# Mamba2 scan and SiLU feed-forward on one core: weight pieces taken up one to three slots ahead, first unit's scan and transposes reordered, one unit's load issued earlier

## Chip, cores and metric

The kernel runs on one core of a Trainium2 chip. The engines are TensorE (PE, matmuls and transposes), VectorE (DVE), ScalarE (ACT), GpSimd (POOL) and SyncE (SP, which issues most loads and stores). The metric is the device time of one execution in microseconds (us); lower is better.

## Reference

```python
# attention: batch 4, heads 8, seq 768, head_dim 32, d_state 16
cum = np.cumsum(log(clip(a)), axis=-1)             # within a chunk
L   = exp(cum[:, None] - cum[None, :]) * causal
y   = ((C @ B.T) * L) @ x + (C @ state) * exp(cum)  # intra + inter chunk
state = exp(sum(la)) * state + sum_j (B_j x_j) * exp(cum_last - cum_j)
# bridge: (batch, heads, seq, head_dim) -> 3072 tokens x 256
h = x @ w_in                                        # 256 x 2048
g = h * (1 / (1 + exp(-h)))                         # SiLU
out = g @ w_out                                     # 2048 x 256
```

Everything is in fp32. The result does not depend on the chunk length, and the kernel uses 64.

## The kernel before

The 3072 tokens are 12 units of 256 (three to a batch entry, `UPB = 3`). A unit first goes through the scan and gives `XM`, the transposed attention output; then through the feed-forward part in slots. `f_s1(g, j)` is a slot of eight fp32 matmul instructions of unit g with two column blocks of w_in, and a silu on ACT that writes `gT`. `f_s2(g, j)` is a slot of eight matmul instructions with w_out, which wants pieces 8 + 2(j mod 4) and 9 + 2(j mod 4) of the weights. In the main loop, group g does `f_s1(g, j)`, one step of the scan of unit g + 1, and `f_s2(g - 2, j)`.

The scan of a unit has these steps: `f_P` (prefix scan of the decays over pa: DVE, POOL, DVE), `f_E` (decay matrix E by one long DVE scan over ab, or for units 0 and 1 `f_Ek`, from a broadcast of ach by matmuls), `f_T` (four PE transposes of B and C into one hp tile, evicted by ACT as bh and ce and by DVE as cw), `f_B` (B times decay, POOL), `f_GD` (grams on PE, then M, the states st and sp on DVE), `f_Y` (output on PE, XM on ACT).

The weights come in 16 pieces of 512 KB, eight of w_in and eight of w_out, through eight raw buffers, and each goes through three steps before it is used: `w_size` (two ACT operations, wu and wv), `w_bits` (two DVE operations on wu, then an add on POOL into wv) and `w_sign` (one DVE operation that writes w_in_sb or w_out_sb, after which SP may issue the load of the piece eight further on). Slot j of f_s1 wants piece j.

Each engine runs its instructions in the order in which the code writes them (the schedule is manual), and the tile framework adds the waits. Two PSUM buffers hold the hp tiles, which f_s1, f_T and the idle matmuls of `busy(n)` share in turn: a third tile waits for the readers of the first. SP issues loads and stores in the order written: after the first loads of units 0, 1 and 2 and of eight pieces come the other eight pieces, then what the main loop asks for (`load_unit`, and the outputs of `f_s2`).

The order around the change is written by hand: a sequence for units 0 and 1, a table `steps` for groups 0 and 1, whose letters s, b and g stand for w_size, w_bits and w_sign of a piece, and three lines in the main loop for group 2:

```python
f_s2(g - LAG, j)
for n in range(2 * j + 10, 2 * j + 12):
    if g == 2 and n < len(W):
        w_size(n)
        w_bits(n)
        w_sign(n)
```

Of the kernel before, what the change touches and what calls it, by code (L numbers as in the profile page):

```python
# [509 lines left out]
```

## Time and profile before

| | before |
|---|---|
| time, median of 3 runs | 430.13 us (429.73 to 430.16) |
| the profiled execution | 429.28 us, of which the span is 427.6 |
| PE busy | 397.3 us, 93% of the span |
| DVE, ACT, POOL busy | 105.9, 105.3, 35.4 us |
| mean granted clock of TensorE | 0.976 |

The span is from the first to the last instruction of the profiled execution. PE busy is no measure of PE at its best, since matmuls are pipelined and their ends are modelled, and a matmul at half clock is busy for twice as long. So stretches of time and the waits in them say more than the shares.

### The profile page before, as it was taken

How to read it: one execution, taken by the hardware profiler on the slowest of the kernel's cores; microseconds unless marked ns; L12 is line 12 of the kernel's file. 1: busy time of each engine (PE TensorE's matmuls, PEld its weight loads, DVE VectorE, ACT ScalarE, POOL GpSimd, SP SyncE). 2: the span in 40 equal slices, each digit the busy share in tenths (PEclk: the TensorE clock that was granted, in tenths of full speed). 3: DMA queues.
4: the chain of work that ended last, by engine and by line, in shares of the span. 5: the costliest groups of instructions: out<-in, count | busy, mean ns of one | idle time of the engine just before them, and what ended most of it. 6: DMA issues, size and time to landing. Idle time of an engine off the chain costs nothing.

```text
span 427.6 us, 7947 instructions
## 1 busy us (share of the span) xinstructions
PE 397.3 (93%) x3478; PEld 328.1 (77%) x3478; DVE 105.9 (25%) x187; ACT 105.3 (25%) x202; POOL 35.4 (8%) x74
## 2 busy tenths in 40 slices
PE   8964998769959999999999999999999999999996
PEld 3443786548838888888888888888888888888885
DVE  5552146543245005005005014023032020000000
ACT  1332355532211222121221222222222222221000
POOL 3122041440000000000000000000000000000000
PEclk9896699999989999999999999999999999999999
DMA  9995149000096044053061071080080000000101
GB/s 174 248 193 165 49 148 161 3 1 14 18 144 81 8 87 51 2 92 44 2 107 30 2 114 24 8 117 14 16 111 14 12 2 14 12 14 0 26 12 25
DMA packets 105966, 25.18 MB, mean 59 GB/s; under 512 B 97228, under 2 KB 101836, under 8 KB 105932
## 3 DMA queue, kind: packets, MB, share of 16 engines
q1 hardware_dynamic: 101772, 24.42, 30.7%
q10 hardware_dynamic: 4160, 0.26, 0.7%
q8 instruction: 27, 0.44, 0.5%
q14 instruction: 7, 0.06, 0.1%
HBM read 21.52 MB, written 3.15 MB: 58 GB/s over the span
## 4 chain that ended last, share of the span: by engine, by line
PE 86%; DVE 5%; POOL 3%; DMA 1%; issue 1%; SPq 1%; ACT 1%; POOLq 0%; ACTq 0%
PE o_ps L391 38%; PE hp L380 37%; POOL wv L154 3%; PE hp L194 2%; PE gy L363 2%; PE gy L306 2%; PE gy L354 1%; PE o_ps L257 1%; DVE w_out_sb L159 1%; PE hp L282 1%; PE gy L312 1%; DVE wu L153 1%; DVE M L317 1%; DMA bct<-in_C_dram 1%; DVE wu L151 1%
## 5 line engine op out<-in xcount | busy, mean ns | idle before, releaser
L380 PE MATMUL hp<-XM,w_in_sb 128*128 128x256 f32 x768 | 185.6, 388 | 11.2 <-DVE w_in_sb L159 10.2
L391 PE MATMUL o_ps<-w_out_sb,gT 128*128 128x256 f32 x768 | 183.3, 384 | 6.9 <-DVE w_out_sb L159 6.7
L380 PEld LDWEIGHTS hp<-XM,w_in_sb 128*128 128x128 f32 x768 | 149.2, 195 | 33.3 <-issue 9.4
L391 PEld LDWEIGHTS o_ps<-w_out_sb,gT 128*128 128x128 f32 x768 | 144.2, 191 | 29.7 <-DVE w_out_sb L159 9.7
L382 ACT ACTIVATE gT<-hp 128x512 f32<-128x512 f32 x96 | 57.3, 597 | 236.3 <-PE hp L380 236.3
L292 DVE TENSOR_TENSOR cw<-hp,pfx 128x256 f32<-128x256 f32 x12 | 5.1, 422 | 149.1 <-ACT ce L291 149.0
L154 POOL TENSOR_TENSOR wv<-wu,wv 128x512 uint32<-128x512 uint32 x16 | 20.2, 1266 | 54.1 <-DVE wu L153 45.5
L250 DVE TENSOR_TENSOR_SCAN E<-ab,diag 128x1024 f32<-128x1024 f32 x10 | 22.9, 2292 | 2.2 <-POOL ab L267 2.2
L317 DVE TENSOR_TENSOR M<-gy,E 128x1024 f32<-128x1024 f32 x12 | 14.7, 1224 | 30.6 <-PE gy L312 30.6
L396 ACT ACTIVATE o_sb<-o_ps 128x256 f32<-128x256 f32 x24 | 9.2, 383 | 52.5 <-PE o_ps L391 52.5
L244 POOL COPY pb<-pa 128x4 f32<-128x4 f32 x12 | 2.3, 191 | 190.6 <-DVE pa L242 190.6
L282 PE MATMUL hp<-ident,bct 128*128 128x128 f32 x48 | 8.6, 297 | 5.0 <-DMA bct<-in_B_dram 4.9
L194 PE MATMUL hp<-idle 128*128 128x512 bf16 x30 | 11.6, 547 | 1.3 <-DVE idle L189 1.3
L282 PEld LDWEIGHTS hp<-ident,bct 128*128 128x128 f32 x48 | 6.4, 150 | 8.1 <-issue 5.5
L334 DVE SCALAR_TENSOR_TENSOR st<-st,pfx,gy 128x64 f32<-128x64 f32 x40 | 11.2, 279 | 1.1
L354 PEld LDWEIGHTS gy<-cw,sp 32*64 32x64 f32 x352 | 6.3, 133 | 6.3 <-issue 5.1
L143 ACT ACTIVATE wu<-raw 128x512 f32<-128x512 f32 x16 | 10.7, 667 | 0.0
L145 ACT ACTIVATE wv<-raw 128x512 f32<-128x512 uint32 x16 | 10.6, 664 | 0.0
L247 DVE TENSOR_TENSOR_SCAN pfx<-pa,pb 128x256 f32<-128x256 f32 x12 | 9.2, 767 | 5.4 <-POOL pa L245 5.4
L369 ACT ACTIVATE XM<-gy 128x512 f32<-128x512 f32 x12 | 7.2, 597 | 13.0 <-PE gy L363 13.0
L363 PE MATMUL gy<-M,xt 64*32 64x64 f32 x768 | 10.3, 224 | 0.0
L291 ACT ACTIVATE ce<-hp,par 128x256 f32<-128x256 f32 x24 | 10.0, 477 | 0.0
(44 smaller groups left out, 117.0 us busy)
## 6 DMA issues: line engine op xcount, KB each, us to landing
ab<-in_a_dram SPq DMA_DIRECT2D x40, 128.0 KB
raw<-in_moe_w_in_dram SPq DMA_DIRECT2D x8, 512.0 KB
raw<-in_moe_w_out_dram SPq DMA_DIRECT2D x8, 512.0 KB
xt<-in_x_dram SPq DMA_DIRECT2D x24, 128.0 KB
out_dram<-o_sb SPq DMA_DIRECT2D x48, 64.0 KB
pa<-in_a_dram SPq DMA_DIRECT2D x12, 128.0 KB
...
```

The source lines that it names most:

```text
L143: nc.scalar.activation(u, raw[n][:, :, :, 1].bitcast(FP32), AF.Abs)
L145: nc.scalar.activation(v, raw[n][:, :, :, 0], AF.Copy, scale=2.0 ** -51, bias=2.0)
L154: nc.gpsimd.tensor_tensor(out=v, in0=u, in1=v, op=ALU.add)
L194: nc.tensor.matmul(out=t, lhsT=idle[:, 0:128], rhs=idle, start=True, stop=True)
L250: nc.vector.tensor_tensor_scan(out=E[u][:, k:k + n].rearrange("p k h t -> p (k h t)"), data0=t, data1=diag[:, 0:n * H].rearrange("p g t -> ...
L282: nc.tensor.transpose(out=tp[:, 2 * i + k], in_=bct[u][:, i, k].rearrange("p h n -> p (h n)"), identity=ident)
L317: nc.vector.tensor_tensor(out=M[u].rearrange("p k g x -> p g k x"), in0=gram[:, :, 0:256].rearrange("p g (k x) -> p g k x", k=2), in1=E[u] ...
L334: nc.vector.scalar_tensor_tensor(out=o, in0=ST[u][:, t], scalar=PFX[u][:, Q * t + Q - 1:Q * t + Q], in1=d, op0=ALU.mult, op1=ALU.add)
L363: nc.tensor.matmul(out=y[32 * q:32 * q + 32, 2 * w + c, 64 * k:64 * k + 64], lhsT=xc[64 * c:64 * c + 64, k, h], rhs=m[64 * c:64 * c + 64, ...
L380: nc.tensor.matmul(out=hp[:, i], lhsT=w_in_sb[:, kc, f * 128:(f + 1) * 128], rhs=xm[:, kc], start=(kc == 0), stop=(kc == KC - 1))
L382: nc.scalar.activation(GTS[g][:, 2 * j:2 * j + 2], hp, AF.Silu)
L391: nc.tensor.matmul(out=OPS[g], lhsT=GTS[g][:, f, 128 * c:128 * c + 128], rhs=w_out_sb[:, f, :], start=(f == 0), stop=(f == NF - 1))
```

## The change

The steps of a piece are written in different slots: the ACT step one to three slots ahead of the sign step, from the table `steps` (now with f_s1 of units 0 and 1 in turn) to the first three slots of group 2 (`late`). f_GD is split into f_G (grams and M) and f_S (states), cw is taken out of f_T as f_C, and the broadcast matmuls out of f_Ek as f_Ab. For unit 0 the prefix scan stands ahead of the scans of E, and the transposes right behind the broadcast matmuls, with fewer idle matmuls (19 instead of 30). ach and sel lie on rows 96 to 107 with zeros in front, so that the broadcast matmuls take 108 rows instead of 12. Unit 3's load is issued before group 2, and unit 4's in slot 2 of it, where it was in slot 7. The scan of unit 3 has its steps in slots 1, 2, 3 and 6 of group 2, where they were in 4 to 7.

```diff
@@ -163,8 +163,9 @@
             load_w(n + RAW, nc.sync)
-    ach = const.tile([S // Q, H, Q], FP32, name="ach")
-    nc.sync.dma_start(out=ach, in_=bass.AP(tensor=a.tensor, offset=a.offset, ap=[[Q, S // Q], [S, H], [1, Q]]))
+    A0, A1 = 96, 96 + S // Q
+    ach = const.tile([128, H, Q], FP32, name="ach")
+    nc.sync.dma_start(out=ach[A0:A1], in_=bass.AP(tensor=a.tensor, offset=a.offset, ap=[[Q, S // Q], [S, H], [1, Q]]))
     load_bc(0, 0, nc.scalar)
     load_bc(0, 1, nc.scalar)
     load_pa(0, nc.sync)
...
@@ -193,11 +194,12 @@
         for i in range(n):
             nc.tensor.matmul(out=t, lhsT=idle[:, 0:128], rhs=idle, start=True, stop=True)
-    sel = const.tile([S // Q, 4, 2, 64], FP32, name="sel")
+    nc.vector.memset(ach[0:A0], 0.0)
+    sel = const.tile([128, 4, 2, 64], FP32, name="sel")
     nc.gpsimd.memset(sel, 0.0)
     nc.gpsimd.affine_select(out=sel, in_=sel, pattern=[[-2, 4], [-1, 2], [0, 64]], compare_op=ALU.not_equal,
-                            fill=1.0, base=0, channel_multiplier=1)
+                            fill=1.0, base=-A0, channel_multiplier=1)
     diag1 = const.tile([128, 1, Q], FP32, name="diag1")
     nc.vector.memset(diag1, 0.0)
...
@@ -251,15 +253,17 @@
                                      data1=diag[:, 0:n * H].rearrange("p g t -> p (g t)"),
                                      initial=0.0, op0=ALU.mult, op1=ALU.add)
+    def f_Ab(u, k):
+        ab[u, k] = t = ps_o.tile([128, H, Q], FP32, name="o_ps")
+        nc.tensor.matmul(out=t.rearrange("p h t -> p (h t)"),
+                         lhsT=sel[:A1, 2 * u + k].rearrange("r c m -> r (c m)"),
+                         rhs=ach[:A1].rearrange("r h t -> r (h t)"), start=True, stop=True)
     def f_Ek(u, k):
-        t = ps_o.tile([128, H, Q], FP32, name="o_ps")
-        nc.tensor.matmul(out=t.rearrange("p h t -> p (h t)"),
-                         lhsT=sel[:, 2 * u + k].rearrange("r c m -> r (c m)"),
-                         rhs=ach.rearrange("r h t -> r (h t)"), start=True, stop=True)
         if k == 0:
             E[u] = sc.tile([128, 2, H, Q], FP32, name="E")
-        scan_E(u, k, 1, t.rearrange("p h t -> p (h t)"))
+        scan_E(u, k, 1, ab.pop((u, k)).rearrange("p h t -> p (h t)"))
     def f_E(u):
         t = ab.pop(u)
...
@@ -289,9 +293,12 @@
         nc.scalar.activation(BH[u], tb, AF.Copy)
         for e in range(2):
             nc.scalar.activation(CE[u][:, e], tcc, AF.Copy, scale=par[:, e:e + 1])
-        nc.vector.tensor_tensor(out=CW[u], in0=tcc, in1=PFX[u], op=ALU.mult)
-    def f_GD(u):
+        TC[u] = tcc
+    def f_C(u):
+        nc.vector.tensor_tensor(out=CW[u], in0=TC.pop(u), in1=PFX[u], op=ALU.mult)
+    def f_G(u):
         first, last = u % UPB == 0, u % UPB == UPB - 1
         bh, ce = BH.pop(u), CE.pop(u)
...
@@ -319,7 +326,13 @@
                                 in1=E[u].rearrange("p k (g e) t -> p g k (e t)", e=2), op=ALU.mult)
         E.pop(u)
         bct.pop(u)
+        DP[u] = gram
+    def f_S(u):
+        first, last = u % UPB == 0, u % UPB == UPB - 1
+        n = 3 if last else 4
+        gram = DP.pop(u)
         if first:
             ST[u] = sc.tile([128, 4, 64], FP32, name="st")
         if not last:
...
@@ -404,75 +417,83 @@
             f_E(u)
         elif plan[j] == "T":
             f_T(u)
+            f_C(u)
             f_B(u)
         elif plan[j] == "G":
-            f_GD(u)
+            f_G(u)
+            f_S(u)
         elif plan[j] == "Y":
             f_Y(u)
+    f_Ab(0, 0)
+    f_Ab(0, 1)
+    f_P(0)
     f_Ek(0, 0)
     f_Ek(0, 1)
+    f_T(0)
+    f_C(0)
+    f_B(0)
+    w_size(0)
+    w_size(1)
+    f_G(0)
+    f_Ab(1, 0)
+    f_Ab(1, 1)
+    w_bits(0)
+    f_S(0)
     busy(6)
-    f_P(0)
-    f_T(0)
-    f_B(0)
+    f_Y(0)
+    w_sign(0)
     busy(4)
-    f_GD(0)
-    w_size(0)
-    w_bits(0)
-    busy(8)
-    f_Y(0)
-    w_size(1)
-    f_Ek(1, 0)
-    busy(6)
-    w_sign(0)
     f_s1(0, 0)
     w_bits(1)
+    f_Ek(1, 0)
+    w_sign(1)
     f_Ek(1, 1)
-    w_sign(1)
+    f_T(1)
+    w_size(2)
+    f_s1(0, 1)
     f_P(1)
-    f_T(1)
+    f_C(1)
     f_B(1)
-    f_s1(0, 1)
-    w_size(2)
-    f_GD(1)
     w_bits(2)
+    w_size(3)
+    f_G(1)
     w_sign(2)
+    busy(4)
     f_s1(0, 2)
-    w_size(3)
+    f_S(1)
     w_bits(3)
+    f_Y(1)
     w_sign(3)
-    f_Y(1)
-    f_s1(0, 3)
-    steps = ((1, 0, "s4"), (1, 1, "b4 s5"), (1, 2, "g4 b5 s6"), (1, 3, "g5 b6 s7"), (0, 4, "g6 b7"), (1, 4, "g7"),
-             (0, 5, ""), (1, 5, ""), (0, 6, "E"), (1, 6, "T s8"), (0, 7, "G b8 s9"), (1, 7, "g8 b9 Y"))
-    for g, j, todo in steps:
-        f_s1(g, j)
+    steps = ((1, 0, "s4"), (1, 1, "b4 s5"), (1, 2, "g4 b5 s6"), (0, 3, "g5 b6 s7"), (1, 3, "g6 b7 s8"),
+             (0, 4, "g7 b8 E"), (1, 4, "g8 s9"), (0, 5, "T b9"), (1, 5, "g9 s10"), (0, 6, "G b10"),
+             (1, 6, "g10 s11"), (0, 7, "Y b11"), (1, 7, "g11 s12"))
+    def w_steps(todo):
         for step in todo.split():
             if step[0] in "sbg":
                 {"s": w_size, "b": w_bits, "g": w_sign}[step[0]](int(step[1:]))
             else:
                 scan_piece(2, 0, step)
-    w_sign(9)
+    for g, j, todo in steps:
+        f_s1(g, j)
+        w_steps(todo)
+    load_unit(3)
+    late = ("b12 g12 s13 b13", "g13 s14 b14", "g14 s15 b15 g15")
     for g in range(2, NU + LAG):
         for j in range(8):
             if g < NU:
                 f_s1(g, j)
             if g + 1 < NU:
-                scan_piece(g + 1, j, ("", "", "", "", "E", "T", "G", "Y") if g == 2 else
+                scan_piece(g + 1, j, ("", "E", "T", "G", "", "", "Y", "") if g == 2 else
                            ("E", "T", "G", "", "", "Y", "", ""))
             f_s2(g - LAG, j)
-            for n in range(2 * j + 10, 2 * j + 12):
-                if g == 2 and n < len(W):
-                    w_size(n)
-                    w_bits(n)
-                    w_sign(n)
+            if g == 2 and j < len(late):
+                w_steps(late[j])
             if g == 2 and j == 2:
-                load_unit(3)
-            if g == 2 and j == 7:
                 load_unit(4)
             if j == 7 and g + 3 < NU:
                 load_unit(g + 3)
```

DVE's rows from the bits step of piece 7 on, in the kernel before (wu, wv and raw are the tiles of a piece, the unit is 2):

```order
L153 TENSOR_SCALAR wu_571<-wu_571 128x512
L159 SCALAR_TENSOR_TENSOR w_in_sb_90<-raw_128,wv_572 128x2x256
L242 TENSOR_SCALAR pa_130<-pa_130 128x256
L247 SCALAR_TENSOR_TENSOR pfx_617<-pa_130,pb0_187 128x256
L266 TENSOR_SCALAR ab_132<-ab_132 128x1024
L250 SCALAR_TENSOR_TENSOR E_621<-ab_132,diag_176 128x1024
L292 TENSOR_TENSOR cw_636<-hp_629,pfx_617 128x256
L317 TENSOR_TENSOR M_682<-gy_653,E_621 128x4x2x128
L334 SCALAR_TENSOR_TENSOR st_433<-st_433,pfx_617,gy_653 128x64 x3
L339 TENSOR_TENSOR sp_687<-st_433,hmask_185 128x256
L151 TENSOR_SCALAR wu_643<-wu_643 128x512
```

The same place in the changed kernel, from the bits step of piece 8 on:

```order
L153 TENSOR_SCALAR wu_570<-wu_570 128x512
L244 TENSOR_SCALAR pa_130<-pa_130 128x256
L249 SCALAR_TENSOR_TENSOR pfx_589<-pa_130,pb0_187 128x256
L270 TENSOR_SCALAR ab_132<-ab_132 128x1024
L252 SCALAR_TENSOR_TENSOR E_593<-ab_132,diag_176 128x1024
L159 SCALAR_TENSOR_TENSOR w_out_sb_91<-raw_330,wv_571 128x512
L299 TENSOR_TENSOR cw_619<-hp_612,pfx_589 128x256
L151 TENSOR_SCALAR wu_602<-wu_602 128x512
L153 TENSOR_SCALAR wu_602<-wu_602 128x512
L159 SCALAR_TENSOR_TENSOR w_out_sb_91<-raw_350,wv_603 128x512
L324 TENSOR_TENSOR M_675<-gy_646,E_593 128x4x2x128
```

The steps of unit 2 stood together behind piece 7 and in front of the bits of piece 8; now pieces 8 and 9 stand between them, with the scan of E in front of the sign of piece 8 and cw behind it.

PE's rows around the transposes of unit 2 (hp is the tile of a slot of f_s1 or of the transposes) in the kernel before:

```order
L380 MATMUL hp_608<-XM_333,w_in_sb_90 128x256 x4
L380 MATMUL hp_623<-XM_511,w_in_sb_90 128x256 x4
L282 MATMUL hp_629<-ident_160,bct_137 128x128 x4
L380 MATMUL hp_647<-XM_333,w_in_sb_90 128x256 x4
L306 MATMUL gy_653<-ce_635,bh_634 64x128 x16
```

And in the changed kernel:

```order
L393 MATMUL hp_606<-XM_327,w_in_sb_90 128x256 x4
L286 MATMUL hp_612<-ident_161,bct_137 128x128 x4
L393 MATMUL hp_629<-XM_497,w_in_sb_90 128x256 x4
L393 MATMUL hp_640<-XM_327,w_in_sb_90 128x256 x4
L313 MATMUL gy_646<-ce_618,bh_617 64x128 x16
```

There was one slot between the transposes and the grams; now there are two, the second of which, f_s1(0, 6), takes the buffer that the transposes had.

SP's loads and stores from the loads of unit 3 on, change against before:

```order
 L98 DMA bct<-in_C_dram 128x8x16 x2
 L105 DMA xt<-in_x_dram 128x8x32 x2
-L399 DMA out_dram<-o_sb 64x256 x4
 L80 DMA pa<-in_a_dram 128x1x256
 L89 DMA ab<-in_a_dram 64x8x64 x4
```

The four stores of group 2's output stood between the loads of unit 3 and those of unit 4; now they stand behind those of unit 4.

## Rows read from the trace of the kernel before

**Rows 1.** Waits of PE: engine, line, who ended them; us in total, times, longest

```profile
PE hp L380 <- DVE w_in_sb L159: 10.2, 3, 5.9
PE o_ps L391 <- DVE w_out_sb L159: 6.7, 5, 1.8
PE hp L282 <- DMA bct<-in_B_dram: 4.9, 2, 4.2
```

**Rows 2.** Windows: us, each engine's busy us (instructions), PEclk, DMA share, GB/s

```profile
18.95:22.36 3.41, 3.41 (x9) 1.87 (x8) 2.52 (x4) 0.60 (x2) 0.71 (x1) 0.50 1.04 389
32.60:39.43 6.83, 3.83 (x12) 2.69 (x16) 1.38 (x3) 0.04 (x1) 1.26 (x1) 0.50 0.71 243
...
42.84:49.67 6.83, 5.93 (x14) 4.81 (x15) 0.69 (x1) 0.60 (x1) 0.03 (x1) 0.50 0.25 77
...
124.76:128.17 3.41, 3.27 (x9) 2.41 (x9) 2.26 (x2) 1.11 (x3) 0.64 (x1) 0.50 0.88 172
128.69:159.57 30.88, 30.88 (x294) 26.54 (x293) 6.69 (x11) 7.15 (x14) 1.06 (x4) 1.00 0.34 56
128.69:427.60 298.91, 294.79 (x2517) 254.00 (x2515) 49.28 (x80) 62.02 (x121) 7.43 (x28) 1.00 0.23 37
```

**Rows 3.** The chain that ended last, one slot: start us, us, what

```profile
97.30 1.73 PE hp L380 x8
```

**Rows 4.** Timeline of the head: start us, us, engine, line, operation [idle before <-releaser]

```profile
2.72 0.41 DVE L184 TENSOR_SCALAR ach<-ach 12x512 f32<-12x512 f32 x1 [1.30 <-DMA ach<-in_a_dram]
...
3.93 3.78 PE L257 MATMUL o_ps<-ach,sel 12*128 12x512 f32 x4
...
10.17 1.06 PE L282 MATMUL hp<-ident,bct 128*128 128x128 f32 x4
...
13.73 1.22 DVE L317 TENSOR_TENSOR M<-gy,E 128x1024 f32<-128x1024 f32 x1 [0.90 <-PE gy L312]
...
16.22 0.42 DVE L151 TENSOR_SCALAR wu<-wu 128x512 f32<-128x512 f32 x1
...
17.85 0.60 ACT L369 ACTIVATE XM<-gy 128x512 f32<-128x512 f32 x1 [4.35 <-PE gy L363]
...
21.23 2.45 PE L380 MATMUL hp<-XM,w_in_sb 128*128 128x256 f32 x8
```

**Rows 5.** Timeline: PE at f_s1(0, 2) and f_s1(0, 3)

```profile
35.59 3.75 PE L380 MATMUL hp<-XM,w_in_sb 128*128 128x256 f32 x8 [5.90 <-DVE w_in_sb L159]
...
43.74 1.62 PE L380 MATMUL hp<-XM,w_in_sb 128*128 128x256 f32 x3 [2.94 <-DVE w_in_sb L159]
```

**Rows 6.** Timeline: one piece of w_out in group 2, and the next one's bits

```profile
75.01 0.42 DVE L151 TENSOR_SCALAR wu<-wu 128x512 f32<-128x512 f32 x1
...
76.03 1.26 POOL L154 TENSOR_TENSOR wv<-wu,wv 128x512 uint32<-128x512 uint32 x1 [1.67 <-DVE wu L153]
...
77.33 0.69 DVE L159 SCALAR_TENSOR_TENSOR w_out_sb<-raw,wv 128x512 uint32<-128x512 uint32 x1 [1.44 <-POOL wv L154]
...
77.94 0.42 DVE L151 TENSOR_SCALAR wu<-wu 128x512 f32<-128x512 f32 x1
```

**Rows 7.** Timeline around the loads of unit 4 (SPq is SP's queue)

```profile
115.90 0.67 SPq L80 DMA_DIRECT2D pa<-in_a_dram  x1
...
117.54 1.89 PE L380 MATMUL hp<-XM,w_in_sb 128*128 128x256 f32 x8
...
123.64 0.30 PE L282 MATMUL hp<-ident,bct 128*128 128x128 f32 x1 [4.21 <-DMA bct<-in_B_dram]
...
128.69 1.89 PE L380 MATMUL hp<-XM,w_in_sb 128*128 128x256 f32 x8
```

**Rows 8.** The page's costliest groups: the first ACT step (busy us, mean ns)

```profile
L143 ACT ACTIVATE wu<-raw 128x512 f32<-128x512 f32 x16 | 10.7, 667 | 0.0
```

**Rows 9.** Timeline: prefix scan and E of unit 3 on DVE, without weights beside it

```profile
96.03 0.29 DVE L242 TENSOR_SCALAR pa<-pa 128x256 f32<-128x256 f32 x1
...
98.26 2.29 DVE L250 TENSOR_TENSOR_SCAN E<-ab,diag 128x1024 f32<-128x1024 f32 x1 [0.22 <-POOL ab L267]
```

More of the change, by code (lines that the diff above doesn't have):

```diff
@@ L183, in f_A @@
     def f_A():
-        nc.vector.tensor_scalar(out=ach, in0=ach, scalar1=1.0, scalar2=1e-6, op0=ALU.min, op1=ALU.max)
-        nc.vector.memset(ach[:, :, 0:1], 0.0)
+        nc.vector.tensor_scalar(out=ach[A0:A1], in0=ach[A0:A1], scalar1=1.0, scalar2=1e-6, op0=ALU.min, op1=ALU.max)
+        nc.vector.memset(ach[A0:A1, :, 0:1], 0.0)
     idle = const.tile([128, 512], BF16, name="idle")
@@ L210 @@
     nc.scalar.activation(tiny, idle[:, 0:1], AF.Silu)
-    busy(6)
+    busy(5)
     f_A()
@@ L234 @@
         pb.append(t)
-    E, M, BT, BH, CE, CW, PFX, ST, DP, XM, GTS, OPS = ({} for _ in range(12))
+    E, M, BT, BH, CE, CW, PFX, ST, DP, XM, GTS, OPS, TC = ({} for _ in range(13))
     def f_P(u):
@@ L406, in scan_piece @@
             f_T(u)
+            f_C(u)
             f_B(u)
         elif plan[j] == "G":
-            f_GD(u)
+            f_G(u)
+            f_S(u)
         elif plan[j] == "Y":
             f_Y(u)
+    f_Ab(0, 0)
+    f_Ab(0, 1)
+    f_P(0)
     f_Ek(0, 0)
     f_Ek(0, 1)
+    f_T(0)
[8 more added lines that the diff above has]
+    f_S(0)
     busy(6)
-    f_P(0)
-    f_T(0)
-    f_B(0)
+    f_Y(0)
+    w_sign(0)
     busy(4)
-    f_GD(0)
-    w_size(0)
-    w_bits(0)
-    busy(8)
-    f_Y(0)
-    w_size(1)
-    f_Ek(1, 0)
-    busy(6)
-    w_sign(0)
     f_s1(0, 0)
     w_bits(1)
+    f_Ek(1, 0)
+    w_sign(1)
     f_Ek(1, 1)
-    w_sign(1)
+    f_T(1)
+    w_size(2)
+    f_s1(0, 1)
     f_P(1)
-    f_T(1)
+    f_C(1)
     f_B(1)
-    f_s1(0, 1)
-    w_size(2)
-    f_GD(1)
     w_bits(2)
+    w_size(3)
+    f_G(1)
     w_sign(2)
+    busy(4)
     f_s1(0, 2)
-    w_size(3)
+    f_S(1)
     w_bits(3)
+    f_Y(1)
     w_sign(3)
-    f_Y(1)
-    f_s1(0, 3)
-    steps = ((1, 0, "s4"), (1, 1, "b4 s5"), (1, 2, "g4 b5 s6"), (1, 3, "g5 b6 s7"), (0, 4, "g6 b7"), (1, 4, "g7"),
-             (0, 5, ""), (1, 5, ""), (0, 6, "E"), (1, 6, "T s8"), (0, 7, "G b8 s9"), (1, 7, "g8 b9 Y"))
-    for g, j, todo in steps:
-        f_s1(g, j)
+    steps = ((1, 0, "s4"), (1, 1, "b4 s5"), (1, 2, "g4 b5 s6"), (0, 3, "g5 b6 s7"), (1, 3, "g6 b7 s8"),
+             (0, 4, "g7 b8 E"), (1, 4, "g8 s9"), (0, 5, "T b9"), (1, 5, "g9 s10"), (0, 6, "G b10"),
+             (1, 6, "g10 s11"), (0, 7, "Y b11"), (1, 7, "g11 s12"))
+    def w_steps(todo):
         for step in todo.split():
```

## Prediction

> **What bounds the kernel now.** I read the page first: TensorE (PE) is busy 93% of a 427.6 us span, so what is left to gain is PE's waits and the stretches in which it runs slowly. Next the waits of PE [rows 1]: 10.2 us for w_in_sb, 6.7 for w_out_sb, and 4.9 for the B load of one unit. Then the windows with the granted clock [rows 2]: 0.50 (1.2 GHz) from 32.60 to 39.43, from 42.84 to 49.67 and from 124.76 to 128.17, each beginning during or right after one of these waits. From 128.69 on the kernel is steady: a unit takes 30.88 us, and 298.91 are left [rows 2]. A slot (eight matmuls) takes 1.73 [rows 3], so the scan steps of a unit cost 30.88 - 16 x 1.73 = 3.2 on PE. All that the change can move lies before 128.69, and the question is when the changed kernel reaches the work that starts there, f_s1(3, 2).
>
> Before that point three places lose time. The head: the first slot starts at 21.23 [rows 4]. The weights: f_s1(0, 2) waits 5.90 and then takes 3.75, f_s1(0, 3) waits 2.94 [rows 5]; in group 2 the slots stand in a cycle of VectorE (DVE) and GpSimd (POOL) for each piece of w_out: bits at 75.01, POOL's add at 76.03, sign at 77.33, the next bits at 77.94 [rows 6], 2.93 a piece. Unit 4: its loads are issued at 115.90, its transposes start at 123.64 although PE's slot of 117.54 was over at 119.3, and the next regular slot starts at 128.69 instead of 117.54 + 2 x 1.73 + 0.44 = 121.4 [rows 7]: 7.2 lost.
>
> **The change, part by part.**
>
> Unit 4's load moves from group 2, slot 7 to slot 2, and unit 3's ahead of group 2. Both then stand on SP's queue in front of group 2's outputs, behind the eight pieces of w_out, the last of which waits for sign 7. By the chain below sign 7 is done at T0 + 15, so both are in long before they are read (unit 4's loads took 8 from issue to first use [rows 7]). Gain 7.2; between 0, if they came late all the same, and 7.2. I take 7.2, since the queue's order settles it.
>
> The head. The transposes of unit 0 move in front of two runs of matmuls on idle data and now follow the two broadcast matmuls of ach. They start between 7.3 (the end of those matmuls less one idle matmul) and 10.17, as now [rows 4]; I take 8.0, near the lower bound, because at 10.17 they wait for no load. From there to M is 3.56 [rows 4], so M starts near 11.5. From M to XM's start is 4.1, and XM takes 0.6 [rows 4]; the bits of piece 0 (0.9 [rows 6]) now stand between M and the state steps, so f_s1(0, 0) starts near 11.5 + 4.1 + 0.65 + 0.9 = 17.2, four earlier than 21.23. The memset of 96 rows of ach lies in the 1.30 that DVE waits for ach's load [rows 4]; were it longer than this wait, the excess would count. The broadcast matmuls read 108 rows where they read 12. No row shows that form; nothing here suggests that rows cost time, and its columns are the same, so 0, or at the most a doubling of about 1 each on a stretch that is no longer the last to end.
>
> From f_s1(0, 0) to the first slot after f_Y(1). Now that is 21.23 to 43.74, 22.5. Of this 10.2 are waits [rows 1], about 2.0 the slow slot at 35.59 (3.75 for 1.73), 0.5 the slow first one, 1.0 the two ach matmuls, which move forward; 0.9 of idle matmuls are new: 9.7 of work. What waits remain? Behind sign 0 DVE has bits 1, scan E, sign 1, scan E, the prefix scan, cw, bits 2, M, sign 2: 0.9 + 1.2 + 0.6 + 1.2 + 1.4 + 0.4 + 0.9 + 1.1 + 0.6 = 8.3. Sign 0 ends near 15.5, so piece 2 is there near 24.5, and PE comes near 23.4: a wait of 1.2; then 0.8 for XM of unit 1. With 9.7 + 2.0 this first slot, T0, starts at 17.2 + 11.7 = 28.9. All this is at full clock. The present head has half rate for long stretches, and the new one has fewer idle matmuls and still short gaps, so I add one stretch at half rate, 1.5: T0 = 30.4 (27.5 with none and a quick head, 33 with three).
>
> Pieces 4 to 15. The three steps of a piece are now in different slots, but look at the order on DVE: sign n stands in front of bits n+1 everywhere, so POOL's add of n+1 cannot start before sign n is done. The cycle is the one of [rows 6], 2.93, whatever slot the steps are written in, and DVE, not PE at 1.73 a slot, paces it. Bits 4 need the first slot (1.73), a silu and the first ACT step, 0.67 [rows 8]: T0 + 3.1. From bits 4 to sign 15's release are 11 cycles and the end of one: 11 x 2.93 + 2.3 + 0.75 = 35.3. Into this row DVE must fit, without PE's help: the prefix scan and E of units 2 and 3, each 4.45 from pa to the end of E (96.03 to 98.26 and 2.2 more [rows 9]), plus 1.0 because POOL's copy for it stands behind an add, less the 1.4 that DVE would have waited for that add: 4.05 each; cw of unit 2, 0.35; M and the states of unit 2, 2.5 (13.73 to 16.22 [rows 4]) and 0.2 of waiting for them. Sum 3.1 + 35.3 + 8.1 + 0.35 + 2.7 = 49.6: the second half of f_s2(0, 3) can run at T0 + 49.6.
>
> Where PE then stands. f_T(2) takes one of two hp buffers; f_s1(0, 6), two tiles on, needs it back, so it waits for cw of unit 2, which stands on DVE behind E of unit 2 and sign 8. PE is there at T0 + 9 x 1.73 + 0.8 = T0 + 16.4; sign 8 starts at 3.1 + 4 x 2.93 + 2.3 + 4.05 = T0 + 21.2, cw is through at 22.3. That is a new wait of 6.0, which the present kernel does not have, since it puts E of unit 2 two slots before the transposes and no weights beside it. It ends in time for DVE's cycle, so it is no term of its own. It brings half rate, though: the present wait of 5.90 was followed by a slot of 3.75 [rows 5] at 0.50 [rows 2]. M of unit 2, on DVE's row, stands behind that slot and the grams, so I add 2.0 (0 if the clock holds, 3.4 if it is low for both).
>
> The Trainium skill (TensorE: Matmul & The Clock Gate, the section on HAM oscillation) says that waits between groups of matmuls put the array back to half rate again and again; it speaks against taking idle matmuls out of the head. [rows 2] agree as far as they go. By it the whole head would run low: the second rival.
>
> **Sum.** After T0 + 49.6 there are half a slot (0.87), 12 slots (20.7), f_Y(3) and f_T(4) with their switches (2.2) to f_s1(3, 2): T0 + 73.4. With T0 = 30.4 and 2.0 for the clock that is 105.8, where the present kernel has 128.69: 22.9 less. Span 105.8 + 298.9 = 404.7. The profiled execution took 429.28 for a span of 427.6, 1.7 around it: 406.4. Its own time lies 0.85 under the median of the runs shown, 430.13, so I say 406.
>
> **Rivals.**
>
> PE bounds it all (10%). If the slot-apart steps do hide the cycle, PE runs from T0 to f_s1(3, 2) without waits: 33 slots (57.0), scans of units 2 and 3 (6.4) and f_T(4) (0.44), 63.9. Then 30.4 + 63.9 + 298.9 + 1.7 = 395, or 393 with no slow stretch. For it: ACT and SP have room, and loads are early. Against it: sign n in front of bits n+1 in DVE's row.
>
> The clock stays at half to 29 us (8%). From the transposes at 8.0 to T0 PE has about 16 of work (three slots 5.2; transposes, grams and outputs of two units 5.7; ach 2.1; 14 idle matmuls 3.0), so far partly beside DVE's. At half rate it becomes the path: with 2 of waits, 9.5 of it are done by 29 and the rest by about 36 to 37. Time 37 + 73.4 + 2.0 + 298.9 + 1.7 = 413. For it: three stretches of 0.50 [rows 2], and eleven idle matmuls fewer. Against it: shorter waits, and four of these are put where PE would wait for piece 2.
>
> Unit 4 still waits for its loads (3%): 406 + 7.2 = 413.
>
> Not faster (2%): the clock stays at half well into group 2. By the same count T0 would be 8 + 2 + 32 = 42. A slot at half rate takes 3.45, longer than DVE's cycle, so PE is the bound: by 80 us it would have done 19 of the 63.9 that follow T0 (the count of the first rival), and the other 45 at full rate, with the last waits for pieces 13 and 15, end at 128, where the present kernel is at that point. So 80 us is where it decides; lower clock for longer is slower than now, and the price is half a microsecond for each at half rate. Against it: in the present profile no stretch after the head is longer than 6.83 [rows 2], and all end once PE runs without gaps.
>
> **How the numbers follow.** The DVE-paced case has 77%, with 399 (T0 27.5, no clock loss: 27.5 + 73.4 + 300.6 = 401.5, and 2 for head steps that I took too long) to 413 (T0 33, 3.4 lost, 2 for steps that I took too short). This range takes in most of the two cases at 413 and leaves out the PE-bound one and the slow one. 0.2% is about what a measurement of this kernel can tell from no change: faster 0.97, same 0.01, slower 0.02.
>
> **What would show it.** Right: the waits of PE name one of 5 to 7 for f_s1(0, 6) ended by cw on DVE, just behind a long E scan; bits of consecutive pieces 2.9 apart from piece 4 on and two gaps of about 7 between pieces 8 and 9 and 13 and 14; no wait for bct; f_s1(3, 2) near 106 and 299 from there to the end. Wrong: pieces less than 2.5 apart (then near 395); a clock of 0.50 over most of the first 30 us (413 or more); a wait of ACT for raw, behind which silu and then PE would stand.

## The result and the profile after

The changed kernel takes **406.85 us** (median of 4 runs, 405.85 to 407.87); the kernel before, run beside it, 429.93 (427.68 to 430.16). The ratio is 0.947 (95% interval 0.943 to 0.951): 23.1 us less, and 0.85 over the 406 predicted. The profiled execution is the longest of the four: 407.87 for a span of 406.2.

From the page of the changed kernel:

```profile
span 406.2 us, 7918 instructions
```

The waits of PE in the changed kernel, which answer to [rows 1] (L393 is f_s1, L404 f_s2, L286 the transposes, L299 cw, L159 the sign step):

```profile
PE hp L393 <- DVE cw L299: 5.7, 1, 5.7
PE o_ps L404 <- DVE w_out_sb L159: 2.7, 2, 1.4
PE hp L286 <- DMA bct<-in_C_dram: 2.0, 1, 2.0
...
PE hp L393 <- DVE w_in_sb L159: 1.1, 1, 1.1
```

The waits for w_in fell from 10.2 to 1.1, those for w_out from 6.7 to 2.7, the wait for B of unit 4 is gone; a wait of 5.7 for cw of unit 2 and one of 2.0 for C of unit 0 are new.

The timeline of the changed kernel at the places that the prediction named. They answer, in order, to [rows 4], [rows 5], [rows 6], [rows 9] and [rows 7]:

```profile
3.56 2.50 PE L259 MATMUL o_ps<-ach,sel 108*128 108x512 f32 x4
...
8.68 0.33 PE L286 MATMUL hp<-ident,bct 128*128 128x128 f32 x1 [1.96 <-DMA bct<-in_C_dram]
...
14.57 1.63 PE L195 MATMUL hp<-idle 128*128 128x512 bf16 x6
...
18.30 1.89 PE L393 MATMUL hp<-XM,w_in_sb 128*128 128x256 f32 x8
...
30.94 14.08 PE L393 MATMUL hp<-XM,w_in_sb 128*128 128x256 f32 x64 [0.74 <-ACT XM L382]
...
40.09 0.42 DVE L151 TENSOR_SCALAR wu<-wu 128x512 f32<-128x512 f32 x1
...
41.15 1.27 POOL L154 TENSOR_TENSOR wv<-wu,wv 128x512 uint32<-128x512 uint32 x1 [1.70 <-ACT wu L143]
...
42.45 0.69 DVE L159 SCALAR_TENSOR_TENSOR w_in_sb<-raw,wv 128x512 uint32<-128x512 uint32 x1 [1.47 <-POOL wv L154]
43.06 0.42 DVE L151 TENSOR_SCALAR wu<-wu 128x512 f32<-128x512 f32 x1
...
50.17 2.29 DVE L252 TENSOR_TENSOR_SCAN E<-ab,diag 128x1024 f32<-128x1024 f32 x1 [0.22 <-POOL ab L271]
...
52.96 0.42 DVE L299 TENSOR_TENSOR cw<-hp,pfx 128x256 f32<-128x256 f32 x1
...
53.43 3.78 PE L393 MATMUL hp<-XM,w_in_sb 128*128 128x256 f32 x8 [5.72 <-DVE cw L299]
...
83.67 1.13 PE L404 MATMUL o_ps<-w_out_sb,gT 128*128 128x256 f32 x4 [1.36 <-DVE w_out_sb L159]
...
105.12 0.60 PE L286 MATMUL hp<-ident,bct 128*128 128x128 f32 x4
...
107.28 1.89 PE L393 MATMUL hp<-XM,w_in_sb 128*128 128x256 f32 x8
```

Read it from below. f_s1(3, 2) starts at 107.28 and not at 128.69 [rows 7], 21.41 earlier; the profiled executions differ by the same 21.41 (429.28 and 407.87), so all of the gain was made before it, and the steady part is unchanged. T0, the first slot behind f_Y(1), is 30.94; the kernel before has 43.74 there [rows 5]. So 12.80 come from the head, and 8.61 from the stretch between T0 and f_s1(3, 2) (84.95 before, 76.34 after). The head takes in weight pieces 0 to 3: all waits for w_in in the kernel before lie in it, and 9.1 of the 12.80 are what these waits fell by (10.2 to 1.1).

The windows of the changed kernel: us, each engine's busy us (instructions), PEclk, DMA share, GB/s.

```profile
11.49:14.90 3.41, 3.41 (x5) 0.98 (x5) 3.27 (x8) 1.24 (x2) 1.26 (x1) 0.50 0.84 95
...
52.45:59.27 6.82, 5.84 (x65) 4.15 (x66) 2.81 (x7) 0.60 (x1) 2.21 (x2) 0.50 0.86 112
```

Two stretches at 0.50 (1.2 GHz) are left where [rows 2] had four; the second follows the wait for cw.

### The profile page after: what moved, and what is told of

It reads as the page before. It is cut to its first block, busy times and chain, and to the rows that moved or that the text cites. A ratio compares the mean times of both kernels' runs of the same rounds, so it can differ in the third digit from the quotient of the medians.

```text
span 406.2 us, 7918 instructions
## 1 busy us (share of the span) xinstructions
PE 386.2 (95%) x3467; PEld 323.6 (80%) x3467; DVE 106.1 (26%) x188; ACT 105.5 (26%) x202; POOL 35.7 (9%) x74
## 4 chain that ended last, share of the span: by engine, by line
PE 84%; DVE 5%; POOL 3%; issue 3%; ACT 2%; DMA 1%; ACTq 0%; POOLq 0%; DVEq 0%
PE o_ps L404 40%; PE hp L393 35%; POOL wv L154 3%; PE gy L376 2%; PE gy L313 2%; PE gy L367 2%; DMA bct<-in_C_dram 1%; DVE w_out_sb L159 1%; PE gy L319 1%; PE hp L286 1%; DVE wu L153 1%; PE o_ps L259 1%; ACT wu L143 1%; DVE wu L151 1%; PE hp L195 1%
## 5 line engine op out<-in xcount | busy, mean ns | idle before, releaser
L393 PE MATMUL hp<-XM,w_in_sb 128*128 128x256 f32 x768 | 182.7, 383 | 8.1 <-DVE cw L299 5.7
L404 PE MATMUL o_ps<-w_out_sb,gT 128*128 128x256 f32 x768 | 181.2, 382 | 2.7 <-DVE w_out_sb L159 2.7
L393 PEld LDWEIGHTS hp<-XM,w_in_sb 128*128 128x128 f32 x768 | 146.6, 192 | 29.9 <-DVE cw L299 6.1
L404 PEld LDWEIGHTS o_ps<-w_out_sb,gT 128*128 128x128 f32 x768 | 143.6, 190 | 23.5 <-DVE w_out_sb L159 3.5
L299 DVE TENSOR_TENSOR cw<-hp,pfx 128x256 f32<-128x256 f32 x12 | 5.1, 423 | 160.7 <-ACT ce L295 160.7
L145 ACT ACTIVATE wv<-raw 128x512 f32<-128x512 uint32 x16 | 10.7, 671 | 0.0
L278 POOL TENSOR_TENSOR BT<-bct,E 128x256 f32<-128x256 f32 x12 | 8.0, 667 | 25.2 <-DVE E L252 17.8
L313 PEld LDWEIGHTS gy<-ce,bh 32*64 32x64 f32 x384 | 5.7, 138 | 5.4 <-issue 4.0
L313 PE MATMUL gy<-ce,bh 32*64 32x128 f32 x384 | 8.8, 293 | 1.2 <-ACT ce L295 1.2
L376 PEld LDWEIGHTS gy<-M,xt 64*32 64x32 f32 x768 | 8.4, 105 | 1.6 <-issue 0.8
```

Of the source, the lines that this page charges most:

```text
L145: nc.scalar.activation(v, raw[n][:, :, :, 0], AF.Copy, scale=2.0 ** -51, bias=2.0)
L313: nc.tensor.matmul(out=gram[64 * c:64 * c + 64, g, 128 * k:128 * k + 128], lhsT=bh[32 * g:32 * g + 32, ts], rhs=ce[32 * g:32 * g + 32, :, ts],
L376: nc.tensor.matmul(out=y[32 * q:32 * q + 32, 2 * w + c, 64 * k:64 * k + 64], lhsT=xc[64 * c:64 * c + 64, k, h], rhs=m[64 * c:64 * c + 64, ...
L393: nc.tensor.matmul(out=hp[:, i], lhsT=w_in_sb[:, kc, f * 128:(f + 1) * 128], rhs=xm[:, kc], start=(kc == 0), stop=(kc == KC - 1))
L404: nc.tensor.matmul(out=OPS[g], lhsT=GTS[g][:, f, 128 * c:128 * c + 128], rhs=w_out_sb[:, f, :], start=(f == 0), stop=(f == NF - 1))
```

## The experiments

Each is an edit of the changed kernel (of the kernel before where it says so). Medians are compared with 406.85; the kernel before, run beside them, gave medians of 428.9 to 430.1 and single runs of 424.5 to 432.3. The changed kernel's four runs are all from one time. So a difference of 1 to 2.5 us between medians of four to six runs says little by itself, and beside it stands the same stretch in the traces: T0 to f_s1(3, 2), 76.34 in the changed kernel.

**1. Unit 4 loaded late again.**

```diff
-            if g == 2 and j == 2:
+            if g == 2 and j == 7:
                 load_unit(4)
```

> The changed kernel, with the loads of unit 4 put back to slot 7 of group 2. Theory (the place of these loads is worth 7.2 us): 414 us, with a wait of PE of 4 to 5 us for B or C of unit 4 and half rate behind it. Rival (the loads would be hidden anyway, the gain came from elsewhere): 407 us and no such wait.

415.84 (415.14 to 416.57), ratio 0.970 (0.964 to 0.976) to the kernel before: 9.0 lost, not 7.2. Timeline, then one window of this kernel:

```profile
110.19 0.45 PE L286 MATMUL hp<-ident,bct 128*128 128x128 f32 x1 [4.16 <-DMA bct<-in_B_dram]
...
112.27 3.62 PE L404 MATMUL o_ps<-w_out_sb,gT 128*128 128x256 f32 x8
```

```profile
109.43:116.26 6.83, 5.53 (x14) 4.00 (x15) 3.41 (x3) 1.11 (x3) 0.76 (x2) 0.50 0.85 148
```

Half rate held for 6.83 about the wait, against 3.41 in the kernel before [rows 2], so that a slot took 3.62. The profiled execution is 8.70 longer than that of the changed kernel, of which 0.75 lie in front of the wait (the slot before it starts at 104.14, in the changed kernel at 103.39): 7.95 are the load's.

**2. The kernel before, with unit 4 loaded early and nothing else.**

```diff
             if g == 2 and j == 2:
                 load_unit(3)
-            if g == 2 and j == 7:
                 load_unit(4)
```

> The kernel before, with the load of unit 4 issued right behind that of unit 3 (at g = 2, j = 2), and nothing else of the change. Theory: the wait of the transposes of unit 4 and the half clock behind it are a gain by themselves, whatever the rest of the change does: late issue in the changed kernel cost 9.0 us (415.84 against 406.85), so early issue alone takes the kernel before from 429.0 to 420 to 422. Rival: in the kernel before, these loads queue on SP behind loads of weights still under way and come no earlier, or the weights come later by it: 427 or more.

422.12 (417.21 to 423.05), ratio 0.984 (0.975 to 0.992): 6.8 less than the 428.91 beside it. The theory, which gave 420 to 422, holds but for 0.1. The timeline of this kernel, T0 and f_s1(3, 2):

```profile
44.84 5.46 PE L380 MATMUL hp<-XM,w_in_sb 128*128 128x256 f32 x12 [2.99 <-DVE w_in_sb L159]
...
122.45 1.89 PE L380 MATMUL hp<-XM,w_in_sb 128*128 128x256 f32 x8
```

From T0 to f_s1(3, 2) it takes 77.61; the changed kernel takes 76.34. So of the 8.61 won there 7.34 are the load of unit 4, and only **1.3 is left for all else that changed behind T0**: the pieces from 4 on taken up ahead and the scans of units 2 and 3 moved. By experiment 1 it is less: with the late load the changed kernel takes 84.38, the kernel before 84.95. What pieces 0 to 3 won is part of the head.

**3. The old head.** The code of the kernel before up to f_Y(1), without f_s1(0, 3), then the steps of the changed kernel; ach stays on 108 rows.

> The changed kernel with the head of the kernel before (units 0 and 1 up to Y of unit 1, with weight pieces 0 to 3 in their old places), then the steps of the changed kernel from slot (1, 0) on. Theory: the first slot behind Y of unit 1 comes at 43.7 as in the kernel before and not at 30.9, all else stays: 406.9 + 12.8 = 419.7, up to 3.4 more if the clock stays at half for the stretch behind it as before. Rival: the pieces, whose loads are there earlier against this later start, then run ahead of PE and the wait of 5.7 for cw of unit 2 goes too: 412 to 415.

414.99 (414.71 to 415.2): 8.1 more, within the 412 to 415 of the rival; but the wait for cw, which the rival had go, is still 5.7, so it came out right for another reason. Two waits of PE in this kernel, then its timeline, with T0 in the last row:

```profile
PE hp L393 <- DVE w_in_sb L159: 8.1, 3, 5.9
PE hp L393 <- DVE cw L299: 5.7, 1, 5.7
```

```profile
3.48 2.79 PE L259 MATMUL o_ps<-ach,sel 108*128 108x512 f32 x4
...
32.19 3.75 PE L393 MATMUL hp<-XM,w_in_sb 128*128 128x256 f32 x8 [5.90 <-DVE w_in_sb L159]
...
38.26 14.08 PE L393 MATMUL hp<-XM,w_in_sb 128*128 128x256 f32 x64 [0.90 <-ACT XM L382]
```

T0 came 7.3 later than in the changed kernel, with 7.0 more of waits for w_in in front of it (8.1 here, 1.1 there): in the old head piece 2 comes late. But T0 also came 5.5 earlier than in the kernel before. Of this 2.1 are the next slot: it is (1, 0) here, which wants piece 0, where the kernel before has (0, 3) and waits 2.94 for piece 3 [rows 5]; the theory of 419.7 had overlooked that. The other 3.4 are there at f_s1(0, 2) already (32.19, and 35.59 in [rows 5]), with the same sequence of head steps. What differs up to there is the 108-row form of the ach product and one idle matmul fewer; the four ach products took 2.79 where they took 3.78 [rows 4]. So I tried the form.

**4. The ach product on 12 rows.**

```diff
-    A0, A1 = 96, 96 + S // Q
+    A0, A1 = 0, S // Q
...
-    nc.vector.memset(ach[0:A0], 0.0)
```

> The changed kernel with the ach product over 12 rows at partitions 0 to 11 as in the kernel before, not over 108 rows. Theory (from the profile of the changed kernel, in which the granted clock is 1.00 from 4.66 on and the first ach products take 2.50 and not 3.78): the broad product is what brings the clock up early; with 12 rows they take 3.78 again, transposes, grams and the second ach products run at half rate, and the time is 1.3 to 4 us longer, 408 to 411. Rival: how many rows a product has is nothing to the clock, and only the order in the head decides it: 406.9 within 0.8, with the clock up at about the same time.

409.16 (408.7 to 410.05): 2.3 more, as the theory has it. The timeline of this kernel, then one row of the kernel of experiment 6, which has 108 rows and the same order up to there:

```profile
3.63 3.75 PE L258 MATMUL o_ps<-ach,sel 12*128 12x512 f32 x4
...
15.55 2.74 PE L195 MATMUL hp<-idle 128*128 128x512 bf16 x6
...
20.59 1.95 PE L392 MATMUL hp<-XM,w_in_sb 128*128 128x256 f32 x8
...
32.38 14.08 PE L392 MATMUL hp<-XM,w_in_sb 128*128 128x256 f32 x64 [0.69 <-ACT XM L381]
```

```profile
15.52 1.77 PE L195 MATMUL hp<-idle 128*128 128x512 bf16 x6
```

Six idle matmuls at 15.55 take 2.74, 0.46 each; in the changed kernel six at 14.57 take 1.63, 0.27 each. The first slot comes at 20.59 and not at 18.30, but T0 only 1.44 later (32.38, 30.94), and the profiled execution is 1.21 longer (409.08, 407.87). (PEclk reads 1.00 here, so the length of the rows and not the column tells the rate so early; the six idle matmuls at 18.80 in the kernel before, in a stretch at 0.50 [rows 2], took 0.44 each.) How early the rate rises varies: in the kernel of experiment 8, with 108 rows, the first four also took 3.75, and six idle ones at 14.35 took 1.46. But in the kernels of experiments 1 and 5 to 9, all with 108 rows and this order up to T0, the six took 1.46 to 1.77, the first slot came at 17.89 to 19.43, and T0 at 30.12 to 31.31. So the form brings the rise forward, by an amount that differs between profiles, and T0 by 1.1 to 2.3. The rows also lie elsewhere (0 to 11 instead of 96 to 107); which of the two counts is not shown.

**5. Bits of a piece ahead of the sign of the one before.**

```diff
-    steps = ((1, 0, "s4"), (1, 1, "b4 s5"), (1, 2, "g4 b5 s6"), (0, 3, "g5 b6 s7"), (1, 3, "g6 b7 s8"),
-             (0, 4, "g7 b8 E"), (1, 4, "g8 s9"), (0, 5, "T b9"), (1, 5, "g9 s10"), (0, 6, "G b10"),
+    steps = ((1, 0, "s4"), (1, 1, "b4 s5"), (1, 2, "b5 g4 s6"), (0, 3, "b6 g5 s7"), (1, 3, "b7 g6 s8"),
+             (0, 4, "b8 g7 E"), (1, 4, "s9"), (0, 5, "T b9 g8"), (1, 5, "s10"), (0, 6, "G b10 g9"),
...
```

> The changed kernel, with bits of piece n+1 ahead of sign of piece n on DVE, from piece 4 to 15; the ACT steps stay where they are. Theory (sign n in front of bits n+1 closes the cycle of 2.93 us): bits of pieces 4 to 8 come about 1.75 us apart, the pace of the slots, the wait for cw falls from 5.7 to about 1, the waits for w_out vanish, 396 us (393 to 399). Rival (DVE and POOL hold each other up when they run side by side, so the cycle stays): bits at least 2.5 apart and 403 us or more.

404.44 (402.72 to 405.06), 2.4 less, where the prediction's own account of the cycle gave 396; T0 to f_s1(3, 2) is 73.90, 2.4 less too. The timeline of this kernel:

```profile
36.38 0.69 DVE L159 SCALAR_TENSOR_TENSOR w_in_sb<-raw,wv 128x512 uint32<-128x512 uint32 x1
36.64 1.56 POOL L154 TENSOR_TENSOR wv<-wu,wv 128x512 uint32<-128x512 uint32 x1 [0.92 <-DVE wu L153]
...
36.99 1.50 DVE L151 TENSOR_SCALAR wu<-wu 128x512 f32<-128x512 f32 x1
...
39.46 1.51 DVE L151 TENSOR_SCALAR wu<-wu 128x512 f32<-128x512 f32 x1
```

The step L151, 0.42 by itself, takes 1.50 beside POOL's add and ends 0.29 after it (38.49, 38.20); the add, 1.27 by itself, takes 1.56 beside the sign step. The two engines hardly work side by side on these steps, and pieces follow each other every 2.47 us, though DVE by itself would need only 1.54 for each (0.42, 0.43 and 0.69). The rival, which said 2.5 or more, is right but for 0.03. The Trainium skill (SBUF — State Buffer, the section "SBUF: two separate sides") says that some operations of VectorE and any of GpSimd share one pair of ports, held for a whole instruction while the other waits; these rows agree in the main: L151 ends 0.29 behind the add, and the add 1.13 behind the sign step (37.07), a little less than the 0.42 and 1.27 that they take alone.

**6. Scan E of unit 2 ahead of bits 4.**

```diff
-    steps = ((1, 0, "s4"), (1, 1, "b4 s5"), (1, 2, "g4 b5 s6"), (0, 3, "g5 b6 s7"), (1, 3, "g6 b7 s8"),
-             (0, 4, "g7 b8 E"), (1, 4, "g8 s9"), (0, 5, "T b9"), (1, 5, "g9 s10"), (0, 6, "G b10"),
+    steps = ((1, 0, "E s4"), (1, 1, "b4 s5"), (1, 2, "g4 b5 s6"), (0, 3, "g5 b6 s7"), (1, 3, "g6 b7 s8"),
+             (0, 4, "g7 b8"), (1, 4, "g8 s9"), (0, 5, "T b9"), (1, 5, "g9 s10"), (0, 6, "G b10"),
```

> The changed kernel, with the prefix scan and E of unit 2 in front of the bits of piece 4, where DVE waits 3.9 us for ACT, not behind the bits of piece 8. Theory (DVE's row of work is the bound and PE's wait for cw is only its shadow, plus half rate behind it): the wait of 5.7 goes, the row is 3.6 us shorter and the 2.5 us in which DVE waits for the slow grams go too: 401 us. Rival (PE pays its waits one by one): 5.7 plus 2 for the clock are won, 399 us. Second rival (piece 4 is what counts and is now later): 407 us.

405.66 (402.75 to 405.75), 1.2 less, no more than the medians of the kernel before differ by, where the theory gave 401. In the traces T0 to f_s1(3, 2) is 74.00, 2.34 less. The timeline of this kernel:

```profile
33.52 2.29 DVE L252 TENSOR_TENSOR_SCAN E<-ab,diag 128x1024 f32<-128x1024 f32 x1 [0.22 <-POOL ab L271]
...
49.84 1.11 DVE L159 SCALAR_TENSOR_TENSOR w_out_sb<-raw,wv 128x512 uint32<-128x512 uint32 x1 [1.48 <-POOL wv L154]
50.88 0.41 DVE L299 TENSOR_TENSOR cw<-hp,pfx 128x256 f32<-128x256 f32 x1
...
51.34 3.78 PE L393 MATMUL hp<-XM,w_in_sb 128*128 128x256 f32 x8 [3.42 <-DVE cw L299]
```

E was ready at 35.8, but in DVE's row cw stands behind the sign of piece 8, and that waits for POOL's add. The wait only fell to 3.4, the 2.3 by which the stretch is shorter, and half rate followed as before. The theory had overlooked that cw queues behind a piece, not only behind E.

**7. Idle matmuls in the wait for cw.** 24 of them, into a tile of ps_o, ahead of f_s1(0, 6):

```diff
     for g, j, todo in steps:
+        if (g, j) == (0, 6):
+            t = ps_o.tile([128, 512], FP32, name="o_ps")
+            for i in range(24):
+                nc.tensor.matmul(out=t, lhsT=idle[:, 0:128], rhs=idle, start=True, stop=True)
         f_s1(g, j)
```

> The changed kernel, with 24 matmuls on idle data (5.2 us) in the wait for cw in front of the slot of unit 0, block 6; they write a tile of the other small PSUM pool. Theory (half rate behind the wait delays M of unit 2 on DVE and so everything after it): the clock stays at 1.00, M comes about 2.5 us sooner and the time is 404.4 us. Rival (the slow slot is hidden beside DVE's row): 407 us, with the clock at 1.00 all the same.

404.6 (404.22 to 405.67), 2.2 less, as expected; T0 to f_s1(3, 2) is 73.81, 2.5 less. The timeline of this kernel:

```profile
47.37 5.34 PE L485 MATMUL o_ps<-idle 128*128 128x512 bf16 x24
...
53.27 1.99 PE L393 MATMUL hp<-XM,w_in_sb 128*128 128x256 f32 x8 [0.56 <-DVE cw L299]
```

The slot starts nearly when it did (53.43) and takes 1.99, not 3.78: the half rate behind this wait costs 2.2 to 2.5 beside the 5.7 of the wait.

**8. No add on POOL.**

```diff
-            nc.vector.tensor_scalar(out=u, in0=u, scalar1=3, scalar2=None, op0=ALU.logical_shift_left)
-            nc.gpsimd.tensor_tensor(out=v, in0=u, in1=v, op=ALU.add)
+            nc.vector.scalar_tensor_tensor(out=v, in0=u, scalar=3, in1=v, op0=ALU.logical_shift_left, op1=ALU.bitwise_xor)
...
-            nc.scalar.activation(v, raw[n][:, :, :, 0], AF.Copy, scale=2.0 ** -51, bias=2.0)
+            nc.scalar.activation(v, raw[n][:, :, :, 0], AF.Copy, scale=-2.0 ** -51, bias=-2.0)
...
-MOST = 2.0 ** 16 * (1.875 - 2.0 ** -22)
+MOST = 2.0 - 2.0 ** -23
```

> The changed kernel with a weight piece taken apart so that the shift and the joining of its low part are one operation of DVE (shift by 3, then exclusive or) and POOL does nothing for it; order unchanged. It holds weights under 2 in size (the reference's are) and rounds some of them by up to 2 in a million otherwise. Theory: the cycle of 2.96 a piece is DVE's bits, POOL's add and DVE's sign one after the other, which can't run side by side; with 0.43 + 0.7 + 0.7 = 1.8 a piece on DVE alone the weights keep ahead of PE, the waits for w_out go, and cw of unit 2 comes 5 us or more earlier: 396 to 399, with cw's wait under 1. Rival: ACT's two passes over a piece and the slots' SiLU (3.1 a slot and piece), or the weights' loads, set the same pace: 403 or more, bits still 2.9 apart.

**396.2** (395.97 to 397.25), ratio 0.927 (0.921 to 0.934): 10.7 less than the changed kernel, as the theory has it. The timeline of this kernel (line numbers one less: L392 is f_s1, L298 cw):

```profile
37.11 0.42 DVE L151 TENSOR_SCALAR wu<-wu 128x512 f32<-128x512 f32 x1
...
37.63 0.69 DVE L153 SCALAR_TENSOR_TENSOR wv<-wu,wv 128x512 uint32<-128x512 uint32 x1
...
38.97 0.42 DVE L151 TENSOR_SCALAR wu<-wu 128x512 f32<-128x512 f32 x1
...
47.45 1.99 PE L392 MATMUL hp<-XM,w_in_sb 128*128 128x256 f32 x8 [0.57 <-DVE cw L298]
...
95.36 1.89 PE L392 MATMUL hp<-XM,w_in_sb 128*128 128x256 f32 x8
```

A piece takes 1.86. The wait for cw is 0.57 with no half rate behind it, no wait for w_out is left, and PE works from T0 (30.12) to f_s1(3, 2) (95.36) in 65.2: the prediction's rival "PE bounds it all" counted 63.9 and 395.

**9. The add's work on DVE as an operation of its own.** Clamp, shift, exclusive or and sign, all on DVE:

```diff
-            nc.gpsimd.tensor_tensor(out=v, in0=u, in1=v, op=ALU.add)
+            nc.vector.tensor_tensor(out=v, in0=u, in1=v, op=ALU.bitwise_xor)
```

> The changed kernel with POOL's add of a weight piece replaced by an exclusive or of the same shape on DVE, as an operation of its own: clamp, shift, exclusive or, sign, all on DVE (weights held under 2 in size, some rounded by up to 2 in a million otherwise). DVE so gets 0.69 more a piece than in the kernel at 396.2, 11 us more in all. Theory: the pace of a piece was the row of DVE and POOL (2.96, of which DVE works 1.55); on DVE alone it is 0.43 + 0.43 + 0.69 + 0.69 = 2.25, so E of unit 2 ends some 5 x 0.7 = 3.5 us earlier than in the changed kernel, cw's wait falls from 5.7 to about 2 with no half rate behind it, and the time is 397 to 399. Rival: the number of DVE's operations is what paces a piece, and the fused operation was what helped: 404 or more.

402.88 (402.13 to 403.31), 4.0 less, between what theory and rival gave; T0 to f_s1(3, 2) is 71.58, 4.8 less. The timeline of this kernel:

```profile
36.68 0.42 DVE L151 TENSOR_SCALAR wu<-wu 128x512 f32<-128x512 f32 x1
...
37.67 0.69 DVE L154 TENSOR_TENSOR wv<-wu,wv 128x512 uint32<-128x512 uint32 x1
...
39.01 0.42 DVE L151 TENSOR_SCALAR wu<-wu 128x512 f32<-128x512 f32 x1
...
50.74 3.78 PE L393 MATMUL hp<-XM,w_in_sb 128*128 128x256 f32 x8 [2.85 <-DVE cw L299]
```

With more work for DVE a piece falls from 2.96 to 2.33, so the hand-over to POOL was the pace, as the theory has it. But the time is 4 more than the theory gave: a wait of 2.85 was left, and half rate came behind it all the same (a slot of 3.78).

**10. The kernel before, with no add on POOL** (the edit of experiment 8).

> The kernel before, its order unchanged, with a weight piece taken apart by DVE alone as in the changed kernel without POOL's add (396.2): weights held under 2 in size, some rounded by up to 2 in a million otherwise. Theory: the new order was needed because POOL's add and DVE's steps of a piece stand in a row. Without the add about 1.7 us a piece fall away, so the waits for w_in (10.2) and w_out (6.7) shrink to a third, while the late load of unit 4 (9) and the old head (8) stay, since neither hangs on the add: 416 to 420. Rival: in the old order a piece's three steps stand behind one another in one slot and ACT's passes, not the add, hold them up: 425 or more.

418.04 (417.21 to 421.72), ratio 0.978 (0.969 to 0.986): 12.1 less, as the theory has it in sum, but not in its parts. The waits of PE in this kernel:

```profile
PE hp L379 <- DVE w_in_sb L158: 8.3, 4, 4.8
...
PE o_ps L390 <- DVE w_out_sb L158: 1.3, 2, 0.7
```

w_out fell from 6.7 to 1.3; w_in only from 10.2 to 8.3, where the theory gave a third and the changed order has 1.1 even with the add. The changed order (23.1 less) and the missing add (12.1 less) nearly add up: 32.7 less with both.

**11. Slot (0, 3) into the wait for XM of unit 1**, on top of experiment 8:

```diff
-    f_Y(1)
     w_sign(3)
+    f_Y(1)
+    f_s1(0, 3)
```

and the steps of pieces 6 to 8 one slot earlier.

> The changed kernel without POOL's add (396.2), with slot (0, 3) right behind Y of unit 1, where PE waits 0.74 for XM of unit 1, and the steps of pieces 6 to 8 one slot earlier to make up for it. Theory: PE is the bound from 30 us on, so every wait of PE that work fills is won in full: 395.5. Rival: piece 3 or the SiLU passes of ACT (1.85 a slot with a piece's two passes, against 1.73 of PE) come late by the same: 396.2 or a little more.

398.12 (397.21 to 399.28), ratio 0.932 (0.927 to 0.938): not faster than experiment 8, and not what the theory gave. The 0.74 is gone, but cw of unit 2 now comes later. One wait of PE, then the first slot:

```profile
PE hp L392 <- DVE cw L298: 2.0, 1, 2.0
```

```profile
19.79 1.89 PE L392 MATMUL hp<-XM,w_in_sb 128*128 128x256 f32 x8
```

1.4 more there than in experiment 8 outweighs the 0.74. But the profiled executions differ by 2.11 (398.10, 395.99), and 1.88 of it stand in front of the first slot (17.91 in experiment 8), where the order is the same: the second ach products took 3.78 here and 3.30 there, so the rate rose later in this profile. So the run shows that the move wins nothing clear, not that it costs 1.9.

## Why the prediction was right, and where it was not

**The sum.** f_s1(3, 2) was put at 105.8 and came at 107.28, with 298.9 from there to the end in both kernels. The profiled execution was 1.5 over the sum made for it (406.4), the median 0.85 over the forecast. The last step to 406 has the wrong sign: a profiled execution that lies 0.85 under the median makes a median of 407.25 from 406.4. That the profiled run of the changed kernel lay over its median, and not under it, is chance.

**The head.** T0 was put at 30.4 (28.9 and one stretch at half rate) and came at 30.94, with one such stretch, from 11.49 to 14.90. That it fits so well is in part luck. The transposes were put at 8.0 "because at 10.17 they wait for no load"; moved forward, they ran into a load that is in by 10.17: the last of them waited 1.96 for C of unit 0 and ended at 9.01. The 8.0 and the 1.06 of [rows 4] make 9.06, so the number held, and M with it (11.42 for 11.5), but what set it was the load. "0, or at the most a doubling" for the 108 rows had the wrong sign: by experiment 4 the broad form wins 1.1 to 2.3 at T0, by an earlier rise of the clock. And the wait for piece 2, 1.13 for 1.2, came from three errors that cancel: 15.5 and 8.3 make 23.8, not the 24.5 written; sign 2 ended at 25.82; and PE came at 24.84, not at 23.4. The first slot, 18.30, was 1.1 later than the 17.2 predicted: the second ach products at half rate (3.55) and ten idle matmuls lie in front of it. The rival of half rate to 29 us fell with the windows: behind 4.66 they have 0.50 for 3.41 of the first 30.9 us.

**Unit 4.** The mechanism was right and the size nearly: 7.2 predicted; 9.0 by the medians and 7.95 by the profiles in experiment 1, 6.8 and 7.34 in experiment 2, according to how long half rate lasts about the wait.

**The pieces.** Bits at 40.09 and 43.06, 2.97 apart for 2.93; the gaps of about 7 at 46.02 to 53.29 (pieces 8 and 9) and 70.30 to 77.24 (13 and 14); the second half of f_s2(0, 3) at T0 + 52.7 for 49.6 + 2.0. The forecast that DVE paces this stretch whatever slot the steps are in held, and experiment 2 shows its consequence: taking up the pieces from 4 on ahead won about 1.3. The waits for w_out fell by 4.0, and the wait for cw brought 5.7. But the reason given, that sign n stands in front of bits n+1, is only half of it. With the order turned round (experiment 5) the time fell by 2.4 and not by 11, since DVE's clamp and POOL's add hold each other up; with the add off POOL (8, 9) the cycle was 1.86 and 2.33.

**The new wait.** 5.72 for 6.0, at f_s1(0, 6), ended by cw just behind a long scan, and 2.2 to 2.5 for the half rate behind it (experiment 7) where I took 2.0. Why the kernel before has no such wait was misread: there E of unit 2 is one slot, not two, ahead of the transposes and ends at 67.94, after they start (65.73); what that place lacks are pieces in DVE's row. "It is no term of its own" is not shown. In experiment 6, 2.30 of the wait went, the waits for w_out stayed at 2.7, and the stretch was 2.34 shorter; but moving the scan also shortens DVE's row. A kernel in which the wait alone goes, say by a third hp buffer, was not run.
